# An FFT convolution: the inverse transform of segments 6 and 7 regrouped over columns

## The chip, the cores and the metric

The kernel runs on one core of a Trainium2 chip. The metric is device time in microseconds (us) of one execution, as a median over several. A core has a matrix engine (TensorE, PE in the profile; its weight loads are PEld), a vector engine (VectorE, DVE), a scalar engine (ScalarE, ACT), GpSimd (POOL) and SyncE (SP), which here only issues DMAs. Sixteen DMA engines move data between device memory, HBM, and the on-chip memory, SBUF. Matmul results land in PSUM, in eight banks, from which DVE or ACT copies them out ("evacuates" them).

## What is computed

A circular 7x7 convolution of a 224x224 picture with 96 channels in and 96 out, by way of the Fourier transform:

```python
def reference(x, w):
    B, H, W, C = x.shape                    # 1, 224, 224, 96
    K = w.shape[0]                          # 7
    wp = jnp.pad(w, ((0, H - K), (0, W - K), (0, 0), (0, 0)))
    Xf = jnp.fft.rfft2(x.astype(jnp.float32), axes=(1, 2))
    Wf = jnp.fft.rfft2(wp.astype(jnp.float32), axes=(0, 1))
    Yf = jnp.einsum('bhwi,hwio->bhwo', Xf, Wf)
    return jnp.fft.irfft2(Yf, (H, W), axes=(1, 2)).astype(jnp.bfloat16)
```

## The kernel before

The kernel does not transform the whole picture. It cuts the height into eight segments of 28 rows (NJ = 8, B = 28). Each segment with its 6 rows of overlap has length L = 34 and is transformed in height alone, into NS = 17 frequencies with a real and an imaginary part, which makes FR = 34 numbers per column and segment. The width is convolved directly, with 7 taps. It is cut into seven tiles of 32 pixels, t = 0 to 6 (TL = 6 is the last). A tile has 16 positions of two pixels, and one position is 2C = 192 numbers per transformed row.

Three kinds of work follow one another for a tile:

- A: the forward transform. Matmuls of input rows (xn) with the matrix Fm, evacuated into xf.
- B: one round per frequency s = 0 to 16 (`b_round`). Some 50 matmuls of xf and J with the transformed weights WF, sums on ACT, DVE and POOL (tt_, u, v) into yf, and every two or three rounds a store of yf into a scratch tensor in HBM, scr.
- C: the inverse transform. scr is read back with the 34 numbers of a segment on the partitions (`load_t`, tile tt), multiplied with the inverse matrix G, evacuated into yo, and yo is stored to the output.

The rounds of tile t run with A jobs of tile t+1 and C jobs of tiles t-2 and t-1 filled in between. `pace` decides how many jobs of a list are due at each of the two fill places of a round. The table CQ says for the tiles 2 to 6 how many C jobs of the older and of the newer tile run there. What is left of tile 5 runs after the last round. The last tile has its own inverse: its scratch is cut into a part scra (9 frequencies) and three parts scrb, which are read back into the xf buffers, and two matmuls (matrices GA and GB) add up in PSUM. Between the GA and GB matmuls sixteen matmuls of wu keep TensorE busy during a wait.

For C, G is a block-diagonal matrix with three blocks: 3 x 34 = 102 rows by 3 x 28 = 84 columns. The eight segments are taken in groups CG of 3, 3 and 2, and the 16 positions in halves h of 8. A group and a half are one tt tile, one yo tile and four matmuls of two positions each (384 columns), 102x84 for the first two groups and 68x56 for the third. That is 24 matmuls and 24 evacuations a tile, in twelve jobs of two. The second job of each group stores yo, lowers the count of held tt tiles, and calls `pump`, which loads the next tt tile if fewer than six are held. `queue_c` at round 3 puts the six loads of the preceding tile in the queue. Each load is issued as two DMAs, one with the largest multiple of 16 rows and one with the rest.

The order is fixed in the program: each engine's instructions stay in the order in which the code issues them (`_Ordered`; therefore all of them carry its line, L82), and so do the DMAs of SP (`dma`, `dorder`), which waits for an instruction's inputs before it issues it, with everything behind it. `evac` gives an evacuation to DVE or ACT by running sums of estimated cost, after the last round in turn (`tail_evac`).

Of the kernel before, what the change touches and what calls it, by code (L numbers as in the profile page):

```python
# [14 lines left out]
B = 28  # L15
# [7 lines left out]
TW = 16  # L23
HALO = 3
PXC = 16
# [10 lines left out]
YBUF = 4  # L36
JGB = ((0, 3), (3, 6), (6, 9), (9, 12), (12, 15), (15, 17))
LAG = 4
CQ = {2: (12, 2), 3: (10, 5), 4: (7, 8), 5: (4, 11), 6: (1, 6)}
NXN = 2  # L40
NP2 = 0
WARM = 16
# [7 lines left out]
def kernel(  # L50
# [7 lines left out]
    _, H, W, C = x.shape  # L58
# [6 lines left out]
    FR = 2 * NS  # L65
# [23 lines left out]
    VE, SE, GE, TE, DE = (_Ordered(e) for e in (nc.vector, nc.scalar, nc.gpsimd, nc.tensor, nc.sync))  # L89
# [6 lines left out]
    def psum_tile():  # L96
        return pools["ps"].tile([128, 2, 512], F32, name="ps")

    def bank():
        return pools["psb"].tile([128, 512], F32, name="pb")  # L100
# [13 lines left out]
    def evac(out_ap, in_ap, n):  # L114
        if tail[0]:
            return tail_evac(out_ap, in_ap, n)
        cv, ca = 180 + 1.0 * n, 160 + 0.85 * n
        if clamp[0]:
            top = max(load.values()) - 2000
            for k in load:  # L120
                load[k] = max(load[k], top)
        if load["v"] + cv <= load["a"] + ca:
            load["v"] += cv
            return VE.tensor_copy(out=out_ap, in_=in_ap)
        load["a"] += ca
        return SE.copy(out=out_ap, in_=in_ap)

    def tail_evac(out_ap, in_ap, n):
        tail[0] += 1
        return VE.tensor_copy(out=out_ap, in_=in_ap) if tail[0] % 2 else SE.copy(out=out_ap, in_=in_ap)  # L130
# [4 lines left out]
    def dorder(r):  # L135
        if dlast[0] is not None:
            tc.add_manual_dep(r.ins, dlast[0].ins.name, NOSYNC, reason="program order")
        dlast[0] = r
        return r

    def dma(out_ap, in_ap):
        r = DE.dma_start(out=out_ap, in_=in_ap)
        if gate:
            tc.add_manual_dep(r.ins, gate[-1].ins.name, SYNC, reason="queue order")
        return dorder(r)
# [7 lines left out]
    G = cpool.tile([3 * FR, 3 * B], BF16, name="Gm")  # L153
# [279 lines left out]
    def a_jobs(t):  # L433
        xf = new_xf(t)
        jobs = []
        for jg in range(2):
            if t == 0:
                jobs.extend(a_bank(t, xf, xh_bufs[jg], 0, 3, jg, 0))
            c = 2 * t + jg
            for h in range(2):  # L440
                for (q, n) in ((0, 3), (3, 3), (6, 2)):
                    jobs.extend(a_bank(t, xf, xn_bufs[c % NXN], h * PXC + 2 * q, n, jg, HALO + h * 8 + q))
            last = jobs.pop()

            def fin(last=last, c=c):
                last()
                if c + NXN < NCH:
                    load_x(c + NXN)
            jobs.append(fin)
        return jobs  # L450
# [134 lines left out]
    tt_tiles = {}  # L585
    puts = []

    def load_t(t, gi, h):
        j0, nj = CG[gi]
        n = nj * FR  # L590
        tt = t_pool.tile([128, TW // 2, 2 * C], BF16, name="tt")
        tt_tiles[(t, gi, h)] = tt
        sv = scr_tiles[t].rearrange("w j s (r e) -> (j s r) w e", r=2)
        n0 = n // 16 * 16
        for (p0, p1) in ((0, n0), (n0, n)):
            dma(tt[p0:p1], sv[j0 * FR + p0:j0 * FR + p1, h * 8:(h + 1) * 8])

    TW2 = 2 * TW * C
    tl_all = xf_bufs[(TL + 1) % 2].rearrange("c p r s w j -> c (p r s w j)")
# [9 lines left out]
    def g_parts():  # L609
# [3 lines left out]
        for j in range(NJ):  # L613
            for i, (s, s1) in enumerate(zip(SL[1:], SL[2:])):
                n = 2 * (s1 - s)
                dma(GB[KO[i] + j * n:KO[i] + (j + 1) * n, j // 4, j % 4 * B:(j % 4 + 1) * B], G[2 * s:2 * s1, 0:B])
                yield

    def c_jobs(t):
        jobs = []  # L620
        for h in range(2):
            for gi in range(3):
                j0, nj = CG[gi]
                hold = {}

                def mk_(q, h=h, gi=gi, j0=j0, nj=nj, hold=hold):
                    def f():
                        if q == 0:
                            hold["yo"] = yo_pool.tile([4 * B, PXC * C], BF16, name="yo")
                        tt = tt_tiles[(t, gi, h)]  # L630
                        yo = hold["yo"]
                        if True:
                            pc = psum_tile() if NP2 else None
                            for b in range(2):
                                pb = pc[:, b] if NP2 else bank()
                                TE.matmul(pb[0:nj * B, 0:4 * C], lhsT=G[0:nj * FR, 0:nj * B],
                                          rhs=tt[0:nj * FR, 4 * q + 2 * b:4 * q + 2 * b + 2, :].rearrange("p w e -> p (w e)"), start=True, stop=True)
                                if not NP2:
                                    evac(yo[0:nj * B, (2 * q + b) * 4 * C:(2 * q + b + 1) * 4 * C], pb[0:nj * B, 0:4 * C], 4 * C)
                            if NP2:  # L640
                              evac(yo[0:nj * B, q * 8 * C:(q + 1) * 8 * C].rearrange("p (b e) -> p b e", b=2), pc[0:nj * B, :, 0:4 * C], 8 * C)
                        if q == 1:
                            w0 = t * 2 * TW + h * PXC
                            dma(out[0, j0 * B:(j0 + nj) * B, w0:w0 + PXC, :].rearrange("h w c -> h (w c)"), yo[0:nj * B])
                            held[0] -= 1
                            pump()
                    return f
                for q in range(2):
                    jobs.append(mk_(q))
        return jobs  # L650

    NTT = 6
    held = [0]
# [3 lines left out]
    def pump():  # L657
        while len(pend) > late[0] and held[0] < NTT:
            load_t(*pend.pop(0))
            held[0] += 1  # L660
# [11 lines left out]
    p0 = prep_jobs(0)  # L672
# [4 lines left out]
    w0 = p0.pop(0)()  # L677
# [3 lines left out]
    p1 = prep_jobs(1)  # L681
# [36 lines left out]
    def add(a, b, jobs):  # L718
        qs.append([a, b, jobs, len(jobs)])
# [49 lines left out]
    load["v"] = load["a"] = 0.0  # L769
    queue_c(0)  # L770
    cj = c_jobs(0)
    gp = g_parts()
    for t in range(2, NT):
# [8 lines left out]
        if t + 1 < NT:  # L782
            add(0, 26, a_jobs(t + 1))
        nold, nnew = CQ[t]
        k1 = 2 * NS if t < TL else 2 * NS - 9
        k0 = 12 if t == 2 else 3
        km = max(13, k0 + -(-(k1 - k0) * nold // (nold + nnew)))
        add(k0, km, cj[:nold])
        cn = c_jobs(t - 1)
        cj = cn[nnew:]  # L790
        add(km, k1, cn[:nnew])
# [4 lines left out]
        for s in range(NS):  # L796
# [12 lines left out]
            if t == TL and s == SA + 1:  # L809
                sv = scr_tiles[(TL, 0)].rearrange("w j s (r e) -> (j s r) w e", r=2)  # L810
# [76 lines left out]
```

## Time and profile before

| | |
|---|---|
| median of 7 runs | 286.96 us (286.29 to 290.4) |
| the profiled execution | 286.96 us |
| its span, first to last instruction | 285.2 us |
| mean granted TensorE clock | 0.982 |
| instructions | 11562 |
| moved by DMA | 46.01 MB, 161 GB/s over the span |
| DMA issues of tt from scr | 72, all on SP |
| DMA issues from yo to the output | 36, all on SP |
| ACT casts from PSUM into yo | 130, 55.9 us busy |

The profile is of one execution. A group's line gives the engine, the operation, the tiles written and read, their shape, the count, then the busy time, the mean duration of one and the idle time before them with what ended it. Matmuls overlap in the array, so a mean of 325 ns does not say that two take 650 ns: for that, one reads the starts in the timeline. The "chain of waits" follows the instruction that ended last back to what released it, step by step. SPq is SP's queue: the time that it takes there to issue a DMA.

### The profile page before, as it was taken

What the parts mean: (1) busy time and instruction counts of PE and PEld (TensorE: products, weight loads), DVE (VectorE), ACT (ScalarE), POOL (GpSimd) and SP (SyncE); (2) the same over time, 40 slices, a digit from 0 to 9 for tenths busy, and PEclk for the clock granted to TensorE, in tenths of its full rate; (3) what the DMA queues carried; (4) which work ended last, traced back from release to release, by engine and by line L of the source; (5) the groups of instructions that cost most, each with busy time, mean ns of one, the idle gap of its engine ahead of it and who ended that gap; (6) DMA issues with size and microseconds to landing.
All of it is one profiled execution on the core that took longest, in us unless ns stands there. A gap on an engine that the chain in (4) does not pass through costs nothing.

```text
span 285.2 us, 11562 instructions
## 1 busy us (share of the span) xinstructions
PE 265.8 (93%) x4822; PEld 237.5 (83%) x4822; DVE 241.9 (85%) x523; ACT 185.4 (65%) x460; POOL 87.7 (31%) x122
## 2 busy tenths in 40 slices
PE   8499998999979889999999999999999999899973
PEld 3299898999979889888989889899989888888652
DVE  6279999999899999988977799778997889988823
ACT  5079885656512856876888767987688875265413
POOL 2741001223423333332243313422332235343300
PEclk9869999999979999999999999999999999999999
DMA  7687142111121369988868772786839832696876
GB/s 165 116 215 198 42 139 78 46 44 44 47 84 44 114 204 188 251 267 250 219 171 234 215 230 92 161 220 200 265 128 209 231 101 84 168 198 198 213 186 192
DMA packets 44492, 46.01 MB, mean 161 GB/s; under 512 B 33458, under 2 KB 35182, under 8 KB 44344
## 3 DMA queue, kind: packets, MB, share of 16 engines
q1 hardware_dynamic: 44024, 43.78, 58.4%
q10 hardware_dynamic: 416, 1.49, 2.2%
q8 instruction: 38, 0.62, 1.0%
q14 instruction: 14, 0.11, 0.1%
HBM read 23.92 MB, written 21.33 MB: 159 GB/s over the span
## 4 chain that ended last, share of the span: by engine, by line
PE 50%; DVE 29%; DMA 10%; issue 6%; POOL 3%; ACT 0%; POOLq 0%; SPq 0%; DVEq 0%; ACTq 0%
PE pb L82 50%; DVE J L82 10%; DVE xf L82 6%; DVE v L82 5%; DMA wq<-in_w_dram 4%; DVE WF L82 3%; DVE yf L82 3%; POOL yf L82 3%; DVE u L82 2%; DMA xf<-scrb 2%; DMA xn<-in_x_dram 2%; DMA tt<-scr 1%; DMA scrb<-yf 1%; POOLq L882 0%; SPq L82 0%
## 5 line engine op out<-in xcount | busy, mean ns | idle before, releaser
L82 PE MATMUL pb<-WF,J 96*128 96x96 bf16 x2898 | 167.4, 207 | 4.7 <-DVE J L82 4.0
L82 PEld LDWEIGHTS <-J 96*128 96x128 bf16 (+1 forms) x2910 | 143.3, 98 | 19.1 <-issue 8.6
L82 POOL TENSOR_TENSOR yf<-v,u 128x384 bf16<-128x384 f32 x75 | 75.3, 1018 | 162.4 <-issue 90.6
L82 ACT CAST xf<-pb 96x408 bf16<-96x408 f32 (+1 forms) x139 | 60.7, 479 | 6.9 <-PE pb L82 4.5
L82 PE MATMUL pb<-WF,xf 96*128 96x96 bf16 x952 | 60.7, 207 | 0.6 <-DVE WF L82 0.6
L82 ACT CAST yo<-pb 84x384 bf16<-84x384 f32 (+1 forms) x130 | 55.9, 479 | 4.5 <-PE pb L82 4.1
L82 DVE TENSOR_TENSOR J<-xf 96x1824 bf16<-96x1824 bf16 (+1 forms) x84 | 57.2, 719 | 0.1
L82 PEld LDWEIGHTS <-xf 96*128 96x128 bf16 x952 | 47.6, 98 | 0.8 <-issue 0.7
L82 PE MATMUL pb<-Fm,xn 118*128 118x136 bf16 x448 | 46.3, 222 | 1.1 <-DVE u L82 0.8
L82 PE MATMUL pb<-tt,Gm 102*84 102x384 bf16 (+1 forms) x144 | 35.6, 328 | 1.2 <-DMA tt<-scr 0.8
L82 ACT CAST WF<-pb 96x480 bf16<-96x480 f32 (+1 forms) x58 | 29.7, 570 | 9.9 <-PE pb L82 9.8
L82 PEld LDWEIGHTS <-xn 118*128 118x128 bf16 x448 | 29.9, 98 | 2.4 <-issue 1.8
L82 PE MATMUL pb<-wq 98*128 98x120 bf16 (+1 forms) x288 | 24.5, 238 | 3.8 <-DMA xn<-in_x_dram 3.7
L82 PEld LDWEIGHTS <-wq 98*128 98x128 bf16 x288 | 21.7, 151 | 4.3 <-issue 4.3
L82 DVE TENSOR_TENSOR J<-J 96x912 bf16<-96x912 bf16 (+1 forms) x42 | 25.0, 595 | 0.0
L82 DVE TENSOR_TENSOR yf<-v,u 128x384 bf16<-128x384 f32 x36 | 20.5, 571 | 1.2
L82 DVE CAST xf<-pb 96x408 bf16<-96x408 f32 (+1 forms) x33 | 15.6, 511 | 0.6 <-PE pb L82 0.6
L82 PEld LDWEIGHTS <-Gm 102*84 102x84 bf16 (+1 forms) x144 | 11.8, 113 | 4.3 <-DMA tt<-scr 1.0
L82 DVE CAST WF<-pb 96x480 bf16<-96x480 f32 (+1 forms) x14 | 8.5, 610 | 5.8 <-PE pb L82 5.3
L82 PE MATMUL pb<-wu 128*128 128x512 bf16 (+1 forms) x48 | 12.0, 415 | 1.0 <-DVE ct L82 1.0
L82 PEld LDWEIGHTS <-wu 128*128 128x128 bf16 (+1 forms) x48 | 5.6, 119 | 7.1 <-issue 3.3
L82 DVE COPY xf<-xf 96x816 bf16<-96x816 bf16 x12 | 9.0, 788 | 0.0
(390 smaller groups left out, 215.7 us busy)
## 6 DMA issues: line engine op xcount, KB each, us to landing
xn<-in_x_dram SPq DMA_DIRECT2D x13, 672.0 KB
scr<-yf SPq DMA_DIRECT2D x30, 288.0 KB
tt<-scr SPq DMA_DIRECT2D x24, 288.0 KB
out_dram<-yo SPq DMA_DIRECT2D x24, 252.0 KB
tt<-scr SPq DMA_DIRECT2D x12, 192.0 KB
out_dram<-yo SPq DMA_DIRECT2D x12, 168.0 KB
scr<-yf SPq DMA_DIRECT2D x6, 192.0 KB
scra<-yf SPq DMA_DIRECT2D x3, 288.0 KB
```

What stands on the lines that cost most here:

```text
L82: r = fn(*a, **k)
```

## The change

The group of two segments no longer takes its 16 positions in halves of 8. Half 0 takes positions 0 to 5 of segments 6 and 7 on 68 partitions, and below them, on 34 more, segment 6 at positions 12 to 15 and segment 7 at 12 and 13: six positions on 102 partitions, three matmuls of 102x84. Half 1 takes positions 6 to 11 of both segments, and segment 7 at 14 and 15 on the third block: one matmul of 102x84 and two of 68x56. A half of this group is now one job of three matmuls and three evacuations. A tile has 22 matmuls in ten jobs.

The third block is loaded by DMAs of its own (`REST`): 34 rows by four positions and 34 rows by two in half 0, 34 rows by two in half 1. The output of this group goes out in three stores in half 0 (56 rows by six positions, 28 by four, 28 by two) and in two in half 1. CQ has new counts, since there are ten jobs in place of twelve. The same C is due in the same rounds as far as ten jobs allow. The dead branches on NP2 (which is 0) are dropped.

```diff
-CQ = {2: (12, 2), 3: (10, 5), 4: (7, 8), 5: (4, 11), 6: (1, 6)}
+CQ = {2: (10, 2), 3: (8, 4), 4: (6, 7), 5: (3, 9), 6: (1, 5)}
...
+    REST = (((6, 12, 16, 0), (7, 12, 14, 4)), ((7, 14, 16, 0),))
...
         n0 = n // 16 * 16
+        w0, w1 = (h * 8, (h + 1) * 8) if gi < 2 else (h * 6, (h + 1) * 6)
         for (p0, p1) in ((0, n0), (n0, n)):
-            dma(tt[p0:p1], sv[j0 * FR + p0:j0 * FR + p1, h * 8:(h + 1) * 8])
+            dma(tt[p0:p1, 0:w1 - w0], sv[j0 * FR + p0:j0 * FR + p1, w0:w1])
+        if gi == 2:
+            for j, wa, wb, q0 in REST[h]:
+                dma(tt[n:n + FR, q0:q0 + wb - wa], sv[j * FR:(j + 1) * FR, wa:wb])
...
+    def c_bank(tt, yo, k, nj):
+        pb = bank()
+        TE.matmul(pb[0:nj * B, 0:4 * C], lhsT=G[0:nj * FR, 0:nj * B],
+                  rhs=tt[0:nj * FR, 2 * k:2 * k + 2, :].rearrange("p w e -> p (w e)"), start=True, stop=True)
+        evac(yo[0:nj * B, k * 4 * C:(k + 1) * 4 * C], pb[0:nj * B, 0:4 * C], 4 * C)
+
+    def put_o(t, yo, p0, j, nj, wa, wb, q0):
+        px = t * 2 * TW + 2 * wa
+        dma(out[0, j * B:(j + nj) * B, px:px + 2 * (wb - wa), :].rearrange("h w c -> h (w c)"),
+            yo[p0:p0 + nj * B, q0 * 2 * C:(q0 + wb - wa) * 2 * C])
...
-                        if q == 1:
-                            w0 = t * 2 * TW + h * PXC
-                            dma(out[0, j0 * B:(j0 + nj) * B, w0:w0 + PXC, :].rearrange("h w c -> h (w c)"), yo[0:nj * B])
-                            held[0] -= 1
-                            pump()
+                        for k in ks:
+                            c_bank(tt, yo, k, 3 if gi < 2 or h == 0 or k == 0 else 2)
+                        if not done:
+                            return
+                        if gi < 2:
+                            put_o(t, yo, 0, j0, nj, 8 * h, 8 * h + 8, 0)
+                        else:
+                            put_o(t, yo, 0, j0, nj, 6 * h, 6 * h + 6, 0)
+                            for j, wa, wb, q0 in REST[h]:
+                                put_o(t, yo, nj * B, j, 1, wa, wb, q0)
+                        held[0] -= 1
+                        pump()
                     return f
-                for q in range(2):
-                    jobs.append(mk_(q))
+                if gi < 2:
+                    jobs.extend((mk_((0, 1), False), mk_((2, 3), True)))
+                else:
+                    jobs.append(mk_((0, 1, 2), True))
```

In the planned order of instructions the inverse matmuls of the rounds of tiles 2, 3, 4 and 5 are 26, 26, 29 and 26 (28, 30, 30 and 30 before), those of tile 6's rounds 14 in both, and 11 follow the last round (12 before). SP has 36 DMAs more. One store changes its place on SP against its neighbours at the end: that of segments 3 to 5 of tile 5's first half stood ahead of the two loads from scra and now stands behind them.

More of the change, by code (lines that the diff above doesn't have):

```diff
@@ L624, in c_jobs, with mk_ @@
                 hold = {}
-                def mk_(q, h=h, gi=gi, j0=j0, nj=nj, hold=hold):
+                def mk_(ks, done, h=h, gi=gi, j0=j0, nj=nj, hold=hold):
                     def f():
-                        if q == 0:
+                        if ks[0] == 0:
                             hold["yo"] = yo_pool.tile([4 * B, PXC * C], BF16, name="yo")
@@ L631, in f @@
                         yo = hold["yo"]
[L632 to L641, printed above, removed]
-                        if q == 1:
-                            w0 = t * 2 * TW + h * PXC
-                            dma(out[0, j0 * B:(j0 + nj) * B, w0:w0 + PXC, :].rearrange("h w c -> h (w c)"), yo[0:nj * B])
-                            held[0] -= 1
-                            pump()
-                    return f
-                for q in range(2):
-                    jobs.append(mk_(q))
+                        for k in ks:
[10 more added lines that the diff above has]
+                        pump()
+                    return f
+                if gi < 2:
+                    jobs.extend((mk_((0, 1), False), mk_((2, 3), True)))
+                else:
+                    jobs.append(mk_((0, 1, 2), True))
         return jobs
```

## The prediction

> **What bounds the kernel now.** I read the busy rows first, then the stretches of the span, then TensorE's timeline around the matmuls that change, then the chain that ended last, and SyncE's queue.
>
> The busy rows (busy us, share of the span, instructions), and the two groups of inverse matmuls (count, busy us, mean ns of one, idle before):
>
> ```profile
> PE 265.8 (93%) x4822; PEld 237.5 (83%) x4822; DVE 241.9 (85%) x523; ACT 185.4 (65%) x460; POOL 87.7 (31%) x122
> ...
> L82 PE MATMUL pb<-tt,Gm 102*84 102x384 bf16 x96 | 23.3, 325 | 1.0 <-DMA tt<-scr 0.8
> L82 PE MATMUL pb<-tt,Gm 68*56 68x384 bf16 x48 | 12.3, 335 | 0.1
> ```
>
> The means are latencies of overlapping matmuls. What one costs the stream is read from starts, below. Busy time by stretch (length, PE, PEld, DVE, ACT, POOL, granted clock, DMA share, GB/s):
>
> ```profile
> 106.00:133.00 27.00, 26.59 (x518) 24.04 (x516) 24.13 (x51) 20.71 (x54) 9.12 (x11) 1.00 0.96 228
> 133.00:162.00 29.00, 28.72 (x545) 25.34 (x542) 24.66 (x52) 23.76 (x61) 9.13 (x10) 1.00 0.80 218
> 162.00:195.00 33.00, 32.94 (x643) 29.95 (x640) 28.88 (x61) 26.04 (x68) 10.84 (x11) 1.00 0.68 184
> 195.00:228.00 33.00, 32.93 (x635) 29.56 (x632) 28.50 (x59) 25.51 (x67) 11.01 (x11) 1.00 0.76 201
> 228.00:245.00 17.00, 17.00 (x346) 15.36 (x344) 15.19 (x33) 9.88 (x26) 7.14 (x7) 1.00 0.31 99
> 245.00:262.00 17.00, 15.66 (x320) 14.18 (x317) 14.87 (x33) 8.80 (x21) 6.61 (x7) 1.00 0.87 188
> 262.00:276.00 14.00, 11.66 (x146) 8.67 (x142) 8.35 (x20) 4.19 (x10) 2.93 (x3) 1.00 0.82 203
> ```
>
> From 106 to 245, where the changed jobs are paced, PE is busy 138.2 of 139 us; DVE never passes 0.90. PE is the bound there. After 245 the DMA share is high and PE has gaps. The end (chain of waits, start and length):
>
> ```profile
> 266.26 2.99 DMA scrb<-yf
> ...
> 269.26 4.94 DMA xf<-scrb
> 274.20 1.83 issue
> 276.04 3.80 PE pb L82 x21
> ```
>
> The last 10 us before 276 are a store and its reload, not PE. So work removed from PE ahead of 245 comes off the span; work removed from the burst after the last round (twelve inverse matmuls from 266.48) does not.
>
> **The change: TensorE.** PE's timeline around a 68-row pair and a 102-row pair:
>
> ```profile
> 144.50 0.34 PE L82 MATMUL pb<-Fm,xn 118*128 118x136 bf16 x3
> 144.77 0.51 PE L82 MATMUL pb<-tt,Gm 68*56 68x384 bf16 x2
> 145.21 0.34 PE L82 MATMUL pb<-WF,J 96*128 96x96 bf16 x4
> ...
> 149.06 0.28 PE L82 MATMUL pb<-Fm,xn 118*128 118x136 bf16 x2
> 149.18 0.49 PE L82 MATMUL pb<-tt,Gm 102*84 102x384 bf16 x2
> 149.50 0.34 PE L82 MATMUL pb<-WF,J 96*128 96x96 bf16 x4
> ```
>
> A Fm matmul takes 0.06 us of the stream (149.06 to 149.18 for two). So the first Fm group is through at 144.68, and the 68-row pair owns 144.68 to 145.21, 0.53 us; the 102-row pair owns 149.18 to 149.50, 0.32 us or 0.16 each. The smaller shape is dearer by 0.21 a pair: a gap before, a wider pitch, and a later start of the next weights.
>
> Here a rule pulls the other way. The Trainium skill, TensorE: Matmul & The Clock Gate, "Back-to-back issue gap", prices a warm matmul by its columns alone (N/2.4 + 2.5 ns: an estimate of 0.16 us for 384 columns), rows not entering. By it only the count matters: 132 for 144, eleven of the twelve in the paced stretch, 11 x 0.16 = 1.8 us. The row says the form matters more, so I take the row.
>
> Before, tiles 0 to 4 have four 68-row pairs each, tile 5 two in its first half: 22 x 0.53 = 11.7 us in the paced stretch. After, the job of half 0 is three 102-row matmuls, 3 x 0.16 = 0.48; that of half 1 one 102-row matmul and one 68-row pair, 0.16 + 0.53 = 0.69. Six of the first and five of the second: 2.9 + 3.4 = 6.3. PE saves 5.4 us, of it 1.8 from count and 3.6 from 17 fewer pairs. The last half of tile 5 goes from 12 to 11 matmuls under the wait to 276; I cost that at nothing. Without that cover it would be worth 0.37 us.
>
> **Evacuations.** Twelve fewer casts of some 0.48 us on ACT or 0.54 on DVE. In the planned order DVE has four fewer instructions, ACT eight. Neither bounds, so nothing gained. But jobs of segments 6 and 7 fill three banks in a row instead of two. The third cast can stand 0.48 us before ACT's next copy, on which DVE's u and v wait. Bounds: nothing, or 11 x 0.48 = 5.3 us if each reached PE. ACT has 7 us free in 162:195 and eight banks rotate: I take nothing, and keep half of the upper end for the range.
>
> **SyncE.** Per tile three loads and three stores more, 36 in all. An issue costs 0.34 us for a plain store to about 0.5 for a small load: some 15 us more on a queue that is often idle. The tightest place:
>
> ```profile
> 246.30 6.93 SPq L82 DMA_DIRECT2D tt<-scr  x12
> 253.33 0.39 SPq L82 DMA_DIRECT2D scra<-yf  x1
> ...
> 260.37 0.99 SPq L82 DMA_DIRECT2D xf<-scra  x2
> 261.45 2.40 SPq L82 DMA_DIRECT2D out_dram<-yo  x1
> ```
>
> Twelve loads become fifteen, so 6.93 becomes about 8.6 and the scra store behind them goes at 255.0 instead of 253.3. The next scra store, at 256.10, waits for its own sum, and the reload at 260.37 waits for that one: covered, with 1 us to spare. The new pace also puts the store of segments 3 to 5 (tile 5, half 0) behind the two xf<-scra loads, once ahead of them. Its yo buffer is wanted only by the last job, under the wait to 276. At the same place one store of 168 KB becomes three of the same bytes, at most two issues of 0.4 us, ahead of a reload that waits until 268.10 anyway.
>
> **DMA engines.** The total is unchanged: 384-byte reads, the same bytes out, in somewhat more pieces. What changes is their spread. In the trace's semaphore records a 96-row load is completed by 16 increments that come with the data, the 84-row stores by 14, the 72-row xf<-scra by 12, a 6-row load by 6. The Trainium skill, DMA: Bandwidth & Descriptors, "Why a DMA increments its semaphore by 16 and not by 1", says why: a DMA uses the largest number of engines up to 16 that divides its slowest dimension, the lowest-numbered ones. No 34-row DMA is in the trace; by that rule it gets two engines. Spread over 16 the new loads would cost nothing; by the rule engines 0 and 1 alone move 68 + 34 + 34 = 136 packets a tile, while the loads of segments 6 and 7 shrink from 80 to 60. They carry 116 packets more a tile. A 384-byte packet took 22 ns at the median, about 40 in the bursts: 2.6 to 4.6 us more of two engines' time per tile of some 29 us.
>
> A load is complete when its slowest engine is, so these two set landings. In the paced stretch the slack covers it: tile 1's first load is issued at 119.57, landed 5.9 us later, and is first read at 135.0, 9.6 us to spare. At 246 there is less. The lag of up to 4.6 us can delay the second scra store's landing, so the reload at 260.37, and the stores and reloads queued behind. The part first read by matmuls at 269 has slack until 276; the scrb reloads have none. Bounds: 0, or 3 us (4.6 less 1.6 of drain before 260). A gain would need a sooner scrb reload, and nothing ahead of it gets smaller. I take 1.
>
> **Sum.** -5.4 + 0 + 0 + 1.0 = -4.4. The profiled execution took 286.96 us (span 285.2), which is also the median of the seven. Forecast 282.6.
>
> **The rivals.**
> 1. Vector and scalar work takes over: with 5.4 us less PE, DVE's share in 162:228 rises from 0.87 to 0.90, and triple evacuations bunch. For: DVE leads the chain for some microseconds near 163 to 171. Against: PE idles almost nowhere in those windows. Half of the PE gain and the same tail: -2.7 + 1.0 gives 285.3. Chance 0.20.
> 2. Slower: the two-engine loads pile up in 106:133, where the DMA share is 0.96 and two tiles' loads fall, 232 extra packets at 40 ns = 9.3 us of lag on engines 0 and 1. It decides from 9.6 us, the slack above; stores of scr, which all 16 engines must land, would hold later loads too. Price: 3 us of PE waiting there, 1.5 at each of three later tiles, 3 in the tail: 10.5 against 5.4, so 292. Against: the lag stays under that slack, and from 120 to 135 the median packet still took 22 ns. Chance 0.13.
> 3. The form's penalty does not go: a triple pays at its edges what pairs paid, leaving the count alone: -1.8 + 1.0, 286.2. The 102-row row speaks against it. Chance 0.07.
>
> **How the numbers follow.** The forecast has 0.60, its own range 281.2 (no tail loss) to 284.6 (tail 3 us). About what a measurement here can tell from no change is 1%: 284.1 and 289.8. Faster by over 1%: most of the forecast, 0.58. Within 1%: the forecast's rest, rivals 1 and 3, 0.29. Slower: rival 2, 0.13. The range 281.2 to 287.5 adds rivals 1 and 3 and the evacuations' half, and leaves out rival 2.
>
> **What would show it.** In count, 120 inverse matmuls of 102x384 (96 before) and 12 of 68x384 (48 before). Each triple of half 0 takes 0.48 us from its first start to the next matmul. PE busy 106 to the end of the paced stretch is still over 0.98 of it, and that stretch is 5.4 us shorter: the scra stores begin near 240.4. From there to the end, 39.5 us before, at most 3 more. PE waits of microseconds on tt<-scr, or landings of scr stores beyond 8 us, would mean rival 2; waits on DVE or on evacuations rival 1. Wrong altogether if 102-row triples take over 0.6 us.

## The result, and the profile after

In a series beside the kernel before, the changed kernel took 286.06 us at the median of 27 runs (283.41 to 289.0), against 287.33 us (64 runs, 285.67 to 290.46). Executions more than 1.5% above the fastest of their kernel count as slow, and the ratios, intervals and mean clocks of this document use the others. The ratio is then 0.9927, with a 95% interval of 0.9907 to 0.9948: a gain of 2.1 us (1.5 to 2.7), where 4.4 were forecast; the medians of all runs are only 1.3 us apart. The sign was right and the range held the time, but half of the gain did not arrive. The profiled execution took 283.80 us, span 282.0, so it is one of the better ones, while that of the kernel before (286.96) is near its median.

From the profile of the changed kernel: the busy rows, and the two shapes of the inverse matmuls (count, busy us, mean ns of one, idle before and what ended it).

```profile
PE 260.8 (92%) x4810; PEld 237.8 (84%) x4810; DVE 240.0 (85%) x519; ACT 182.0 (65%) x452; POOL 87.5 (31%) x122
...
L82 PE MATMUL pb<-tt,Gm 102*84 102x384 bf16 x120 | 29.6, 325 | 2.6 <-DMA tt<-scr 1.0 <-DVE u L82 0.8 <-ACT yo L82 0.6
L82 PE MATMUL pb<-tt,Gm 68*56 68x384 bf16 x12 | 3.1, 336 | 0.0
```

The counts are those forecast, 120 and 12. New is what stands behind the last bar of the first row: these matmuls now wait for DVE's u (0.8) and for ACT's yo (0.6). The same stretches as before (length, PE, PEld, DVE, ACT, POOL, granted clock, DMA share, GB/s):

```profile
133.00:162.00 29.00, 28.48 (x557) 26.27 (x555) 24.59 (x52) 23.26 (x60) 9.87 (x10) 1.00 0.69 196
162.00:195.00 33.00, 32.25 (x647) 30.18 (x645) 28.70 (x60) 26.11 (x68) 10.98 (x12) 1.00 0.74 208
228.00:245.00 17.00, 16.25 (x346) 15.14 (x342) 16.46 (x35) 7.96 (x20) 6.06 (x6) 1.00 0.43 133
262.00:276.00 14.00, 11.65 (x58) 7.72 (x56) 7.32 (x17) 4.69 (x11) 0.00 (x0) 0.88 0.80 220
```

In 162:195 PE is idle for 0.75 us where it was idle for 0.06, with DVE's load as before. In the last stretch the granted clock is 0.88; it was 1.00 (the changed kernel is some 4 us further on there). The end of the chain of waits (start, length):

```profile
242.56 3.37 DMA tt<-scr
246.06 12.26 PE pb L82 x254
258.32 8.33 DMA out_dram<-yo
267.25 5.25 PE pb L82 x21
272.51 3.88 PE pb L82 x22
```

Before, the last links ahead of PE were a store to scrb and its reload. Now it is a store to the output, the very one that the new pace moved behind the two xf<-scra loads. The chain follows the wait that ended last, and two ended almost together here: in the semaphore records the last reload of scrb landed at 272.37, 0.14 us ahead of the first GB matmul. Which of the two counts is taken up with the fifth series.

The span of both profiles by stage, in us. The marks are the activation of a round on ACT (tt__), the first matmul with GB, and the last instruction:

| stage | before | after |
|---|---|---|
| start to tile 2's first round | 103.24 | 102.63 |
| tiles 2 to 5 | 135.94 | 132.42 |
| tile 6, first to last round | 26.96 | 26.49 |
| last round to first GB matmul | 9.90 | 10.96 |
| GB matmuls to the end | 9.21 | 9.49 |

So 3.5 us are gained in the paced tiles, 0.5 in tile 6, and 1.3 are given back behind the last round. The first row has nothing of the change in it.

### The profile page after: what moved, and what is told of

Same layout as the page of the kernel before. It is cut to its first block, busy times and chain, and to the rows that moved or that the text cites. A ratio compares the mean times of both kernels' runs of the same rounds, so it can differ in the third digit from the quotient of the medians.

```text
span 282.0 us, 11570 instructions
## 1 busy us (share of the span) xinstructions
PE 260.8 (92%) x4810; PEld 237.8 (84%) x4810; DVE 240.0 (85%) x519; ACT 182.0 (65%) x452; POOL 87.5 (31%) x122
## 4 chain that ended last, share of the span: by engine, by line
PE 51%; DVE 30%; DMA 10%; issue 4%; POOL 2%; SPq 0%; ACT 0%; DVEq 0%; POOLq 0%; ACTq 0%
PE pb L82 51%; DVE J L82 10%; DVE xf L82 7%; DVE v L82 5%; DMA wq<-in_w_dram 4%; DVE WF L82 3%; DVE yf L82 3%; DMA out_dram<-yo 3%; DVE u L82 2%; POOL yf L82 2%; DMA xn<-in_x_dram 2%; DMA tt<-scr 1%; SPq L82 0%; DVE tt L82 0%; ACT yo L82 0%
## 5 line engine op out<-in xcount | busy, mean ns | idle before, releaser
L82 ACT CAST yo<-pb 84x384 bf16<-84x384 f32 (+1 forms) x121 | 51.6, 483 | 9.4 <-PE pb L82 7.2
L82 PE MATMUL pb<-tt,Gm 102*84 102x384 bf16 (+1 forms) x132 | 32.2, 326 | 2.6 <-DMA tt<-scr 1.0
L82 PEld LDWEIGHTS <-wq 98*128 98x128 bf16 x288 | 21.2, 151 | 4.4 <-issue 4.3
L82 DVE CAST xf<-pb 96x408 bf16<-96x408 f32 (+1 forms) x32 | 15.0, 510 | 0.5 <-PE pb L82 0.5
L82 PE MATMUL pb<-wu 128*128 128x512 bf16 (+1 forms) x48 | 13.1, 444 | 1.0 <-DVE ct L82 1.0
L82 PEld LDWEIGHTS <-wu 128*128 128x128 bf16 (+1 forms) x48 | 6.4, 136 | 7.3 <-issue 2.5
```

What stands on the lines that cost most here:

```text
L82: r = fn(*a, **k)
```

## Where PE's saving stays

For each profile I took the starts of consecutive matmuls from the first tt load to the first scra store, and charged each a nominal pitch (0.0426 us for a WF matmul, 0.06 for Fm, 0.161 for an inverse one). What a 68-row pair takes beyond that I call the form; the rest is waiting.

```
                     length   inverse at 0.161   form   waiting
before               138.57        19.32         4.22     2.80
after                135.06        17.71         1.08     3.80
```

Form and count give 3.1 + 1.6 = 4.7 us, and 1.0 comes back as waiting (the rest, 0.2, is where the border falls among the WF matmuls). One of these waits, PE's timeline of the changed kernel first, then DVE's at the same time (start, length, what; in brackets the idle time before):

```profile
173.46 0.33 PE L82 MATMUL pb<-tt,Gm 102*84 102x384 bf16 x1
174.54 0.32 PE L82 MATMUL pb<-tt,Gm 102*84 102x384 bf16 x1 [0.75 <-DVE u L82]
```

```profile
172.27 1.40 DVE L82 TENSOR_TENSOR J<-xf 96x1824 bf16<-96x1824 bf16 x2
173.59 0.62 DVE L82 TENSOR_TENSOR J<-J 96x912 bf16<-96x912 bf16 x1
174.14 0.34 DVE L82 SCALAR_TENSOR_TENSOR u<-pb,tt__4563 128x192 f32<-128x192 f32 x1
```

The second matmul needs a PSUM bank. A bank comes free when DVE has read it for u, and u stands behind three J planes, which take 1.9 us. PE has got through its work earlier, and so stands before the same DVE work. DVE as a whole is no busier than it was; it is the order within one round that binds. A wait of 0.74 to 0.94 us at this place (174 to 176 us) is in 13 of the 14 profiles with the new groups, e8's being the exception, and in none of the six with the old ones.

## The experiments

Ratios are to the kernel before on the same chip in the same series, with a 95% interval. There were five series on four chips, the first two on one.

**First series: the parts of the change, one at a time.** e1 is the kernel before with all three blocks of Gm in the matmuls of the group of two (84 columns, the last 28 zero over its 68 rows). The group keeps its matmuls and its DMAs; only the shape is the same as that of the others. e2 is the same edit in the changed kernel.

```diff
-TE.matmul(pb[0:nj * B, 0:4 * C], lhsT=G[0:nj * FR, 0:nj * B],
+TE.matmul(pb[0:3 * B, 0:4 * C], lhsT=G[0:nj * FR, 0:3 * B],
```

> The kernel before, with the third group's weights taken as 68 rows by all 84 columns of G (the last 28 are zeros) in place of 68x56: 24 matmuls a tile, no DMA changed. Form theory (what counts is the switch between the 56-column form and the others): PE's pair takes 0.32 us instead of 0.53, 22 pairs x 0.21 = 4.6 us less PE work in the rounds. If nothing else binds, ratio 0.984, and a span of about 280.6. Bank theory (PE runs into PSUM banks that DVE frees late): the saving of PE is there in the pitch, but some 1 to 2 us come back as PE waits on DVE; ratio 0.987 to 0.991. DMA theory (the loss of the changed kernel sits in its 36 added DMAs): here there are none, so the full 4.6, and clearly below the changed kernel's 0.993. If columns don't matter and rows do, no change: 1.000.

> The changed kernel with 84 columns for its last five 68x56 pairs too. Form theory: five switches less in the rounds, 5 x 0.21 = 1.05 us, ratio 0.9927 - 0.0037 = 0.989. Bank theory: about half of that or nothing, 0.991 to 0.993. DMA theory: 0.989, and behind the kernel before with wide weights by what the added DMAs cost, though it has two matmuls a tile less (1.8 us in its favour).

e1: 288.12 us, ratio 1.0005 (0.9971 to 1.004). In its profile the form falls from 4.22 to 0.21, and tiles 2 to 5 are 2.3 us shorter (133.66), so the penalty belongs to the 56 columns and not to the 68 rows. But in this profile the tile-6 rounds took 29.94 us in place of 26.96, and that ate it. PE's timeline in e1, and its stretches:

```profile
245.94 0.34 PE L82 MATMUL pb<-WF,J 96*128 96x96 bf16 x4 [0.75 <-DVE J L82]
...
248.76 0.83 PE L82 MATMUL pb<-tt,Gm 102*84 102x384 bf16 x2 [1.21 <-DMA tt<-scr]
```

```profile
244.00:248.30 4.30, 2.80 (x62) 2.50 (x58) 3.88 (x8) 0.82 (x2) 1.09 (x3) 1.00 0.82 198
248.30:255.20 6.90, 6.44 (x69) 5.89 (x70) 4.43 (x9) 2.52 (x6) 1.93 (x2) 0.51 1.28 201
255.20:262.00 6.80, 6.80 (x140) 6.35 (x139) 5.33 (x12) 4.80 (x12) 1.71 (x2) 1.00 0.40 135
```

PE stood still for 2 us within four, and then ran 6.9 us at a granted clock of 0.51: 69 matmuls where the next 6.8 us have 140. By the clock that is some 3.4 us lost, behind 2 us of waiting. The waiting alone does not bring it on: e16 waited 0.75 and 1.28 us at the same place, and kept the full clock there.

e2: 283.59 us, 0.9862 (0.9816 to 0.9909), six runs. The last 1.03 us of form go, 0.63 come back as waiting.

e3 is the kernel before with its loads of the group of two split as the changed kernel's are: six positions as before, the last two of each segment as 34-row DMAs, four more a tile.

```diff
+        nw = 8 if gi < 2 else 6
-            dma(tt[p0:p1], sv[j0 * FR + p0:j0 * FR + p1, h * 8:(h + 1) * 8])
+            dma(tt[p0:p1, 0:nw], sv[j0 * FR + p0:j0 * FR + p1, h * 8:h * 8 + nw])
+        if gi == 2:
+            for j in range(nj):
+                dma(tt[j * FR:(j + 1) * FR, nw:8], sv[(j0 + j) * FR:(j0 + j + 1) * FR, h * 8 + nw:(h + 1) * 8])
```

> The kernel before, computing the same, with the loads of its third group split as the change splits them: six positions on 64 and 4 rows, and two positions of each segment as a 34-row DMA: 24 loads more, 136 packets a tile on two engines, the same bytes. DMA theory: slower by 1 to 1.5 us, ratio 1.003 to 1.005, and all of it from the first scra store on. Bank theory: 1.000, PE's waits in the rounds unchanged. If the two-engine loads reached the rounds too: 1.01 and waits on tt<-scr.

288.93 us, 1.0054 (1.0019 to 1.0089). Tiles 2 to 5 lengthen by 0.4 us (136.33), and no PE wait of microseconds on tt<-scr appears there. Behind the last round there is no loss (8.10 + 9.06). In its profile too, a half-clock stretch (250.5 to 257.3) lies in tile 6's rounds, which last 30.35 us and so leave the DMAs more time before the end. The loss of 1.5 us is of the size that the DMA theory gave, but not at its place; its cause is not shown. In the semaphore records of the changed kernel, each 34-row load is completed by two increments that come with the data, so it does get two engines; each took at most 0.7 us longer to land than the mean of the 16-engine loads on either side of it.

e4 is the changed kernel with tile 5 taken as before: its old groups, loads and stores, and `CQ[6] = (1, 6)`.

> The changed kernel with tile 5 (the last that takes this path) grouped and loaded as before, tiles 0 to 4 as changed. DMA theory: the last tile's share of the span (first scra store to the end) returns from 40.3 to about 39.4 us, while the rounds keep their gain, so 0.9 us better less 0.6 of PE work: ratio 0.991 to 0.992. Bank theory: the tail costs nothing, so only the 0.6 us of PE comes back: ratio 0.995.

283.58 us, 0.9864 (0.9821 to 0.9907), six runs; last round to GB 9.47 us in place of 10.96. It is better than either theory gave, and pointed to the end.

**Second series: pace and sums.** e5 is the changed kernel again. In e6 it queues tile 5's loads one round earlier (`s == (2 if t == TL else 3)`). e7 is e1 with the same earlier queue, so that e1's wait on tt<-scr should go. e8 puts all sums of tiles 2 to 5 on POOL, to take them out of DVE's way:

```diff
-bool(now) if t < TL else s >= NS - 2 or (s < 12 and bool(now))
+False if t < TL else s >= NS - 2 or (s < 12 and bool(now))
```

> The changed kernel once more, on the same chip as the three below, so that they can be compared with it. Clock theory (where TensorE's clock is granted at half speed differs between runs; the trigger is PE's wait of some 2 us at the loads of tile 5, early in the last tile's rounds): its runs spread from 283.4 to 287, faster ones with full clock through the last tile's rounds. Ratio 0.9927 as before, median 284 to 286.

> The changed kernel with the loads of tile 5 put in SyncE's queue one round earlier (round 2 of the last tile in place of 3), so that PE does not wait for them. Clock theory: PE's wait of 1.0 us on tt<-scr goes, and with it the half clock in the rounds of the last tile in those runs that had it: median 283 or less, spread small, ratio 0.985. DMA theory: only the wait of 1.0 us itself goes at most, ratio 0.989 to 0.990, and the spread stays. Bank theory: nothing but that 1.0 us either.

> The kernel before with wide weights (as in e1) and the loads of tile 5 one round earlier. e1 had 2.3 us less in its rounds and gained nothing. Clock theory: its profile had half clock from 248.3 to 255.2, at a price of 3.4 us, because PE stood still for about 2 us just before; without that wait the gain of the rounds appears: ratio 0.987 to 0.990. If the lost gain of e1 has another cause: 0.996 to 1.000.

> The changed kernel with the yf sums of the rounds that also make J done on POOL and not on DVE, in tiles 2 to 5: DVE loses 20 sums of 0.57 us just where it holds u and v back (it gets about ten evacuations in exchange). Bank theory: PE's idle time in the rounds (3.8 us before the first scra store; 2.8 in the kernel before) falls by 1 us or more, ratio 0.989. DMA and clock theory: no change there, 0.9927. If POOL's sums come too late for their stores or get in DVE's way: slower.

e5: 285.44, 0.9903 (0.9867 to 0.9938). e6: 284.59, 0.9907 (0.988 to 0.9933), no gain over e5 (its profile is of its slowest execution). e7: 285.97, 0.9878 (0.9807 to 0.9949), with 26.28 us in tile 6's rounds in its profile: without the wait on the loads and the half clock, e1's saving gets through them. But the ratio rests on two of its six runs (281.47 and 285.60 us), so that e1's saving reaches the end is suggested, not shown. e8: 284.55, 0.99 (0.9861 to 0.9938); the wait at 173 goes, others come, waiting is 3.82 in all. One DVE instruction more or less is not the lever.

**Third series: rests, wide Gm, sixteen engines.** e9 exchanges the two halves' rests in tile 5 (one store fewer ahead of the reload of scrb), e10 adds the wide Gm to it, e11 adds the wide Gm to e4, and e12 issues each 34-row load as 32 and 2 rows, so that it is spread over 16 engines:

```diff
-                dma(tt[n:n + FR, q0:q0 + wb - wa], sv[j * FR:(j + 1) * FR, wa:wb])
+                for r0, r1 in ((0, 32), (32, FR)):
+                    dma(tt[n + r0:n + r1, q0:q0 + wb - wa], sv[j * FR + r0:j * FR + r1, wa:wb])
```

> The changed kernel, in tile 5 alone with the third blocks of the two halves exchanged: half 0 now stores in two pieces and half 1, after the last round, in three. So one DMA fewer stands between the second xf<-scra load and the last scrb store. Slot theory (the DMAs take eight semaphores in turn, and the last scrb store, the ninth after that load, waits until the load has landed): the store is issued about 2.3 us after the start of the last round in place of 4.4 to 4.9, and the stretch from there to the GB matmuls returns from 11.0 to 12.3 to about 10; ratio 0.984 to 0.988. Bandwidth theory (the tail's DMA queues are simply fuller): no change in that stretch, ratio 0.991 to 0.993. PE does one 68x56 pair more in the rounds, 0.2 us.

> The same with 84 columns of G for all pairs. Form and slot theory together: 1.0 us less PE work in the rounds, of which bank waits take about half, so 0.5 us better than the run before it: ratio 0.982 to 0.987, the best of all. Clock theory: a denser PE may meet a half-speed stretch at the start of the last tile's rounds; then its runs spread by 3 us and the median gains nothing.

> Tile 5 grouped as in the kernel before (twelve loads, single stores) and 84 columns of G everywhere. No slot wait and the fewest DMAs in the tail: slot theory 0.983 to 0.987, equal to the run before it. If the tail's cost is in the loads (two engines, fifteen issues) rather than in the slot, this one is better than that run by 1 us.

> The changed kernel with each 34-row load cut into 32 rows, which go to sixteen engines, and 2 rows: the lag of engines 0 and 1 is gone, 18 DMAs more are issued. Two-engine theory (1 us of the tail as predicted): better by up to 1 us, ratio 0.989. If the two engines never were late (their loads landed within 0.7 us of their neighbours in the changed kernel's trace): the same or worse by the issues, 0.993 to 0.996.

e9: 288.55, 1.0014 (0.9975 to 1.0054). e10: 286.47, 0.997 (0.9935 to 1.0005). e11: 285.96, 0.9905 (0.9866 to 0.9943). e12: 289.37, 1.0047 (1.0012 to 1.0083). All four are above what was expected of them, and the series has no run of the changed kernel itself, so part of this may lie in the chip. e12 gives no support to the two engines as the cause: with the loads spread over 16, and 18 DMAs more, nothing is won. e9 and e10 leave the moved store where it is, and PE's wait on ACT's yo behind the last round stays (1.6 and 3.6 us). e9's profile lost most elsewhere, in work that its edit doesn't touch:

```profile
218.76 0.86 PE L82 MATMUL pb<-tt,Gm 102*84 102x384 bf16 x2 [2.47 <-DMA tt<-scr]
```

```profile
217.80:224.60 6.80, 5.84 (x59) 5.25 (x60) 2.50 (x5) 2.90 (x7) 0.99 (x1) 0.50 0.85 206
```

Again a wait on loads, then 6.8 us at half the clock. These are tile 4's loads. The first of them had landed 0.5 us ahead of its use in the profile of the changed kernel (1.3 before).

**Fourth series: is it the number of DMAs on SP?** From tile 2's to tile 6's first round SP issues 153 DMAs before and 182 after, 77 and 98 us of issue time. e15 adds 36 copies of two rows by four numbers to the kernel before, into a tile that nobody reads, at the places of the added DMAs (`extra(n)` issues n of them). e13 moves 28 other small copies, those of Gm into GA and GB, from SP to POOL in the changed kernel; e14 does so in the kernel before; e16 is the changed kernel again.

```diff
+        if gi == 2:
+            extra(2 - h)
...
-            dma(GA[j * 2 * SA:(j + 1) * 2 * SA, j * B:(j + 1) * B], G[0:2 * SA, 0:B])
+            GE.dma_start(out=GA[j * 2 * SA:(j + 1) * 2 * SA, j * B:(j + 1) * B], in_=G[0:2 * SA, 0:B])
```

> The changed kernel, with the 28 small copies of Gm into GA and GB (one a round in tiles 3 and 4) issued by POOL instead of SP. Theory SP (the 36 DMAs more make SP late and pass the lateness on to tile 4's loads and to the last stores): SP's issue time from tile 2 to tile 5 falls from 98 us to below 82, PE does not wait on tt<-scr at the start of tile 5's rounds, ratio to the kernel before 0.986 or less, at least 0.004 below the changed kernel as it stands in this batch. Theory PE alone (the return is all in PSUM banks and clock, SP has time to spare): no difference from the changed kernel beyond 0.003.

> The kernel before with the same move, as a control. Theory SP: before, tile 4's loads land 1.6 us ahead of their first use and no store of the end waits for a semaphore, so that relief of SP is worth nothing here: ratio 0.998 to 1.002. If the move to POOL helps for another reason (fewer DMAs on SP at all, or POOL's queue), this run gains as much as the changed kernel does: 0.996 or less. If POOL's issue work delays its sums, both become slower.

> The kernel before with 36 copies of 2 rows of 4 numbers of Gm (into a tile that nobody reads), on SP at the places of the changed kernel's added DMAs: two or one behind each load and each store of the group of two segments. PE's, DVE's and ACT's work, the loads and stores are the kernel's own. Theory SP (the number of DMAs costs, by issue time and by waiting for a semaphore that an earlier DMA holds): SP's issue time from tile 2 to tile 5 goes from 77 us to above 88, the last stores wait on semaphores as in the changed kernel, ratio 1.004 to 1.010. Theory PE alone, or theory load (it is the two engines of the 34-row loads): within 0.002 of 1.

> The changed kernel as it stands, beside the other three on the same chip: 0.990 to 0.994 by its three series so far. It is the bar for the run with the copies on POOL.

e13: 286.37, 0.9993 (0.995 to 1.0035). e14: 289.38, 1.007 (1.0038 to 1.0103). e15: 287.65, 1.0006 (0.9976 to 1.0036). e16: 286.22, 0.9958 (0.9919 to 0.9996). My theory of a late SP fails here. e15 has SP's 98 us of issue time, and by its interval loses at most 0.36%, about 1 us, and most likely nothing. So the number of DMAs does not explain e3 either, which has fewer. e13 brings SP to 74 us, below the kernel before, and is slower than e16, not faster. POOL is the worse place for the copies, by 0.3 to 0.7%; why, I did not follow up. Against its own control, 0.9993 / 1.007 = 0.9924, the change gains with them on POOL what it gained in the first comparison (0.9927), and no more than 0.3% beyond e16, which the intervals don't resolve.

**Fifth series: the moved store alone.** e17 is the changed kernel with six of tile 5's jobs in tile 6's rounds instead of five. On SP this changes one thing, the store of segments 3 to 5 stands ahead of the xf<-scra loads again (with which the DMAs behind it come to use other completion semaphores, see below); on PE two matmuls come forward from behind the last round. e18 adds the wide Gm.

```diff
-CQ = {2: (10, 2), 3: (8, 4), 4: (6, 7), 5: (3, 9), 6: (1, 5)}
+CQ = {2: (10, 2), 3: (8, 4), 4: (6, 7), 5: (3, 9), 6: (1, 6)}
```

> The changed kernel with six jobs of tile 5 in tile 6's rounds instead of five (CQ of 6: (1, 6)). This puts the store of segments 3 to 5 (tile 5, half 0) back ahead of the two xf<-scra loads, and two matmuls from behind the last round into the rounds; nothing else moves on SP. Theory tail (the moved store holds its yo buffer and a semaphore into the end): ACT and PE no longer wait for out_dram<-yo or for yo behind the last round by more than 0.5 us, last round to the first GB matmul 9.5 us or less (11.0, 12.3 and 13.0 in three profiles of the changed kernel), ratio 0.986 to 0.990. Theory PE alone (the tail loss is chance of one execution): as the changed kernel, 0.991 to 0.996.

> The run before with all three blocks of Gm for every matmul of the inverse (84 columns instead of 56 for the 68-row pairs, too), so that no pair of another shape is left. If both effects add: 0.003 below the run before, 0.983 to 0.988, the best version. If PSUM banks take it back: the same as the run before.

PE's timeline behind the last round, the changed kernel:

```profile
263.81 1.14 PE L82 MATMUL pb<-tt,Gm 102*84 102x384 bf16 x4 [0.61 <-ACT yo L82]
264.89 0.69 PE L82 MATMUL pb<-xf,GA 72*112 72x384 bf16 x3
267.25 1.34 PE L82 MATMUL pb<-xf,GA 72*112 72x384 bf16 x5 [1.67 <-ACT yo L82]
268.38 4.12 PE L82 MATMUL pb<-wu 128*112 128x384 bf16 x16
```

and e17:

```profile
263.11 1.75 PE L82 MATMUL pb<-tt,Gm 102*84 102x384 bf16 x9
264.92 2.72 PE L82 MATMUL pb<-xf,GA 72*112 72x384 bf16 x8
267.48 2.76 PE L82 MATMUL pb<-wu 128*112 128x384 bf16 x16
271.72 0.99 PE L82 MATMUL pb<-xf,GB 128*112 128x384 bf16 x5 [1.48 <-DMA xf<-scrb]
```

In the changed kernel PE waits for banks that ACT cannot empty into yo, and then the sixteen wu matmuls take 4.12 us, most of them at half the clock, up to the GB matmuls at 272.51. (In e4 and e15 they take 4.44, with no such wait before them.) In e17 neither wait is left; the burst takes 2.76 us and has 1.48 us of slack ahead of the reload. ACT, in the changed kernel, and SP's queue there:

```profile
266.73 0.47 ACT L82 CAST yo<-pb 56x384 bf16<-56x384 f32 x1 [1.83 <-DMA out_dram<-yo]
```

```profile
257.20 1.03 SPq L82 DMA_DIRECT2D xf<-scra  x2
258.32 5.26 SPq L82 DMA_DIRECT2D out_dram<-yo  x4
263.63 0.48 SPq L82 DMA_DIRECT2D xf<-scrb  x1
266.00 0.35 SPq L82 DMA_DIRECT2D scrb<-yf  x1
267.99 1.67 SPq L82 DMA_DIRECT2D xf<-scrb  x2
```

and in e17:

```profile
258.02 1.04 SPq L82 DMA_DIRECT2D xf<-scra  x2
259.15 3.58 SPq L82 DMA_DIRECT2D out_dram<-yo  x3
262.96 0.33 SPq L82 DMA_DIRECT2D xf<-scrb  x1
264.98 0.35 SPq L82 DMA_DIRECT2D scrb<-yf  x1
```

The store issued at 258.32 landed 8.33 us later, behind the two reloads, and held its yo buffer until 266.65; ACT's last cast waited for that. A wait of PE on ACT's yo behind the last round is in all nine profiles that have the moved store (0.7 to 3.6 us; e6 apart, whose queue in tile 6 is another), and in none of the ten without it.

But PE's burst has to be over only when the last reload of scrb lands, and that reload is late, too. SP's queue in the kernel before, and a line of SP's waits in the changed kernel (256 to 275 us: in total, times, longest):

```profile
268.46 0.52 SPq L82 DMA_DIRECT2D scrb<-yf  x1
```

```profile
SPq L82 <- DMA xf<-scra: 1.8, 1, 1.8
```

In these records the DMAs of SP and ACT use eight completion semaphores in turn, and none goes out before the earlier one with its semaphore has landed. In the changed kernel the last two scrb stores, one on ACT's queue and one on SP's, take those of the two xf<-scra loads. In the kernel before they take others; in e17, one place on, SP's store takes that of the first load and ACT's neither. In us from the start of the last round, from the issues and the semaphore records:

| | before | changed | e5 | e16 | e17 |
|---|---|---|---|---|---|
| first xf<-scra load landed | -1.06 | 1.22 | 2.57 | 3.21 | 0.40 |
| ACT's scrb store issued | 0.12 | 1.30 | 2.65 | 3.28 | 0.13 |
| second xf<-scra load landed | 1.68 | 4.38 | 4.88 | 5.41 | 2.98 |
| SP's scrb store issued | 2.33 | 4.44 | 4.94 | 5.47 | 2.21 |
| its reload, the last, landed | 9.82 | 10.82 | 12.11 | 11.68 | 8.83 |
| first GB matmul | 9.90 | 10.96 | 12.25 | 12.95 | 8.96 |

The data of SP's store are ready at 2.2 to 2.4. In seven profiles (the changed kernel's, e2, e5, e8, e12, e13, e16) it goes 0.06 or 0.07 us after the second load has landed. The first GB matmul follows the last reload within 0.14 us in each column but e16's, so there the wait for yo costs nothing of its own. In e16 it does, 1.3 us, and that wait, too, is mostly one for a semaphore: ACT stands at its scrb store, with the casts behind it.

```profile
266.02 1.61 ACT L82 CAST yo<-pb 84x384 bf16<-84x384 f32 x4 [3.32 <-DMA xf<-scra]
```

From the last round to the first GB matmul the ten profiles with the moved store take 9.65 to 13.64 us, 11.2 at the mean, and the ten without it 8.10 to 10.70, 9.5 at the mean. The semaphore is not the whole of it: in e9 SP's store takes that of the first load and goes at 3.13, and the last reload still lands at 10.76.

In time, e17 took 284.78 us, 0.9923 (0.9892 to 0.9954), and e18 284.86, 0.9922 (0.9887 to 0.9957), both short of what I expected. The profiled execution of e17 took 282.73 us, near the forecast for the change; the series did not. So the cause of the waits behind the last round is shown, but its worth over many runs is not: e17 and e18 together are 0.7 us below the changed kernel at the mean, on other chips. By ratio e2 and e4 are the best (0.986, six runs each, one chip), but e11, which joins them, had 0.9905 on another chip; none is clearly better than the changed kernel.

**The granted clock, over all runs.** Each run has its mean granted clock. Within one kernel, a run with 0.01 less takes 0.89 us longer (291 runs, each series against its own mean; the slope's standard error is 0.1). This accounts for a quarter of the spread within a kernel. The means:

```
                                   runs   us       clock
before, in the five series          119   287.19   0.9811
changed kernel, its three series     43   285.37   0.9766
e17 and e18                          17   284.64   0.9748
```

The changed kernel runs at a clock 0.0045 lower, which by that slope is an estimated 0.4 us. This mixes chips: beside the kernel before of its own series e5's clock is 0.002 higher and e16's 0.006 lower, so the 0.4 is not certain. e17 and e18 are 0.010 below the kernel before of their own series (0.985), by the slope 0.9 us. One stretch of 3.4 us at half speed is 0.006 of a span, so this is one or two such stretches more per execution. Why there are more of them is not shown.

## Why the prediction came out half right

- **TensorE, 5.4 us: right, with its place slightly off.** Form and count were 5.4 together; up to the first scra store, which has 15 of the 17 pairs and 10 of the 11 matmuls, they measured 4.7 where 4.8 were due. The other 0.6 belongs to tile 6's rounds, and that stage is 0.5 shorter. Each triple of half 0 took 0.49 us, where I had said 0.48. The formula of the Trainium skill (TensorE: Matmul & The Clock Gate, "Back-to-back issue gap") would have given 1.8. It knows only the 384 columns that stream through, and the page gives it for a matmul by itself and says that in a stream it is too high for many columns; here the 102-row matmuls took the 0.16 us that it gives, and the 68-row ones more. The row was the right choice, and e1 shows that the difference is in the columns of the weights. "The scra stores begin near 240.4" put all of it ahead of that store and left no room for waits; they began at 241.66.
- **Evacuations at nothing: the step that failed first.** I looked at the third cast on ACT, and kept its cost in the range but not in the sum. What came was DVE: u frees a bank, and u stands behind the J planes. Waiting rose by 1.0 us in the pair of profiles; in e4, e5, e8, e13, e16 and e17 it was 3.8 to 4.2, in e3, e14 and e15 3.2 to 3.7, so that 0.6 to 1.0 is a fair size. I had the mechanism as rival 1, with DVE's rising share as its sign. In 162:195 the share stayed at 0.87; the sign to look at was the order of u behind J within one round.
- **SyncE, "covered": right for the number of DMAs, wrong for their order.** They cost 21 us of issue time between the first rounds of tiles 2 and 6, where I had 15 for all, and e15 shows no loss from that. But I wrote of the moved store "its yo buffer is wanted only by the last job, under the wait to 276". That is the second step that failed: I followed the buffer and took the end of that wait as fixed. It ends with the last reload of scrb. With the moved store SP's scrb store waits for the semaphore of an xf<-scra load and goes 2.1 us later, counted from the last round, and the reload lands 1.0 us later, and the GB matmuls with it. To the end that makes 1.3 us in the profile, and 2.6 and 3.1 in e5's and e16's. The reload of scra, "covered, with 1 us to spare", came later as well: 22.1 us after tile 6's first round, 21.2 before. e15 has 22.2 there without a loss behind the last round (9.47): SP's scrb store has the first load's semaphore there, and that is free in time.
- **DMA engines, 1 us in the tail: a wrong cause, and the nearly right size is luck.** The 34-row loads do get two engines, as the rule of the Trainium skill (DMA: Bandwidth & Descriptors, "Why a DMA increments its semaphore by 16 and not by 1") has it. Neither e3's end nor e12 shows a lag from it at the place I named. The loss there comes with the moved store. Whether the small loads cost something elsewhere, as e3's 1.5 us may mean, is open.
- **The sum.** -5.4 + 1.0 (banks) + 1.3 (behind the last round) is -3.1. The stages from tile 2 on give -2.7 in the two profiles; 0.4 is not accounted for, and 0.6 more of their difference of 3.2 lies in the start. Over the runs of the table above the difference is 1.8 us. The first profile is of a fast execution; e16's is at its median time, gains 3.6 us from tile 2 to the last round and gives 3.1 back behind it. That the end explains the rest of the runs in the same way is likely, but not shown, since e17's time did not follow its profile. My lower end of 281.2 was a slip: without a loss in the tail the sum gives 281.6.
- **The rivals.** By the ratio the change makes 284.9 of 286.96; rival 1's 285.3 is nearest to that, by half of its own mechanism. Rival 3's 286.2 is next to the median of 286.06, which is luck. Rival 2 did not come: in 106:133 PE is busy for 26.63 us as before (26.59), and the one wait on tt<-scr in the profile is 1.0 us, 0.8 before. Rival 3 is excluded by the form's fall from 4.22 to 1.08.

What stays open is why tile 4's loads come late in some executions (between 190 and 240 us PE waits on tt<-scr in 7 of the 20 profiles, once in a relative of the kernel before, and there for 0.4 us), what starts a stretch of half clock, and what taking away the waits at the end is worth over many runs.

## What to carry to other kernels

When a buffer's last reader moves behind a long transfer on a queue, follow the buffer, not only the queue: its next writer, and everything that stands behind that writer. Where completion semaphores are used in turn, ask also which earlier transfer each store behind it now has to wait for. A wait that covers a cost is itself the end of a chain; see whether the change lengthens that chain. Where PE is the bound by a hair, price a saving on PE against the next engine's order inside one round, since its busy share can stay the same while PE begins to wait for it. And before tuning away a theory such as "too many DMAs", add the suspected cost alone to the old kernel: it is one run.

## What was not expected of the hardware

- A pair of matmuls with 56 columns of weights between others of 84 or 128 costs 0.53 us of the stream, and with 84 columns over the same 68 rows about the 0.32 us of the others. Zero columns were free: e1's form fell from 4.22 to 0.21 us.
- A DMA can wait for a completion semaphore with its data ready. The changed kernel's scrb store at 266.00 takes the one that the second xf<-scra load had (issued 257.56, landed 8.37 us later, at 265.93), and its data were ready at 263.9. One store more or fewer ahead of it changes which slow transfer it stands behind.
- The granted clock falls to half in stretches of 3.4 or 6.8 us. After 2.0 us of PE waiting in e1 and 2.5 in e9 such a stretch followed, and it cost more than the wait. After as much waiting in e16, at the place of e1's, none did.
